# Weight squares in tiles of their own, weight blocks requested earlier, and TensorE in source order through the first down projection

## The chip, the core and the metric

One Trainium2 chip, one of its cores. The metric is the time in device microseconds of one execution of the whole program. The engines are named as the profile names them: PE (TensorE matmul), PEld (its weight loads), DVE (VectorE), ACT (ScalarE), POOL (GpSimd) and SP (SyncE, which here only issues DMAs).

## The reference

Windowed causal attention with a linear distance bias for 8 batches of 8 heads (576 positions, 64 dimensions), and then a bilinear feed-forward layer over the 4608 tokens that come out of it (512 channels, 1536 hidden). In short:

```python
scores = (q @ k.T) / sqrt(64) - slope[h] * |i - j|      # where 0 <= i - j < 128, else -1e9
attn   = exp(scores - max) ; attn /= attn.sum(-1) + 1e-9
x      = (attn @ v) transposed to (4608, 512)
out    = ((x @ w_a) * (x @ w_b)) @ w_out                # w_a, w_b: (512, 1536), w_out: (1536, 512)
```

The three weights come as float64 and everything else as float32. The result is wanted nearly as exact as float32, so the kernel writes the operands of most large products as a high and a low float16 part and takes three products (high x high, high x low, low x high). Each operand is first multiplied by a power of two, or near one, that is worked out from sums of squares.

## The kernel before

**Two streams.** One stream is the feed-forward work of a batch: `up` (the products with both up weights and their elementwise product, the tile `h`) and then `down` (the product with `w_out`). The other is the attention of the next batch, in pairs of heads, four pairs a batch. `att.along(main, n, place)` interleaves the two: after each step of the main stream it advances the attention to a place in proportion. Batch 0 differs: its attention runs first and alone (`first_attention`), then come `first_up` (49 steps) and `first_down` (24 steps), beside which the attention of batch 1 runs.

**The weights.** They pass through a third stream, `weights`, a generator advanced in small steps by whoever is in charge: 1.5 steps per step of the first attention, 50 in steps 0 to 39 of `first_up`, 12 in the first 12 steps of `first_down`, and the rest behind it. One chunk is two blocks of 512 KB; there are 12 chunks of up weights and 6 of `w_out`. For each chunk:

- `load_weights` issues two DMAs from SP (L121) into one of three raw places (`raws`, which lie in the tile `wdn`, not yet used for its own data).
- `convert` turns the 64-bit words into float32 on DVE in three operations (L132, L134, L135). The result goes to one of nine places in the tile `wsum`.
- `squares` (ACT, L141) writes the squares as bfloat16. Up to now they go over the raw words of the same chunk, so the raw place stays taken until the squares have been read.
- For an up chunk, `up_norms` sums the squares on PE (L157, `wn_ps`), `up_scales` makes the scales, and `split_up` (ACT L149, DVE L150) writes the two float16 parts to `wup`. The load of chunk n+3 is written behind `up_norms` of chunk n.
- For `w_out`, the sums of squares are added up, cast (DVE L102) and summed over the partitions by one matmul (PE L103, `wtot`). From that DVE makes `ratio` (L227), and only then are the 12 blocks split into `wdn`, high part on ACT (L231) and low part on DVE (L232). All products of `first_down` read `wdn`.

**The attention of one pair.** `scores` (PE into `sc_ps`: L380 for batch 1, L384 for later ones), the maximum with the bias (DVE L388) and the exponential (ACT L389), then `normalize`, which writes the probabilities as two float16 parts into the one tile `phl` (ACT L405, DVE L406), then `transpose_probs`, a transposing DMA from SP into `pT` (L411), then `pv` (PE L507 into `x_ps`, which `keep_x` empties on ACT at L420). `lay_out_qk` issues four copies on SP (L352 to L355) that bring a pair's split queries and keys into the places from which `scores` reads them. `load_v` (SP, L273) brings the values of a whole batch.

**What sets the order.** The scheduler arranges each engine's instructions by a simulation of its own, unless an engine is under `manual_schedule`; then they stay in the order in which the source issues them. Before, SP is manual through `first_attention` and all of `first_batch` (which holds `first_up`, `first_down` and the weights), and PE is manual from batch 1 on. `first_down` has four accumulating PSUM banks open at once (`dn_ps`, PE L818), and each of its first 12 steps gives 12 products to them.

```python
weave(att.along(first_up(st, h), 49, 3.2), (weights, 0, 40, 50))
weave(att.along(first_down(0, out_scale(st), h), 24, 5.15), (weights, 0, 12, 12))
```

Of the kernel before, what the change touches and what calls it, by code (L numbers as in the profile page):

```python
# [13 lines left out]
BF16 = mybir.dt.bfloat16  # L14
# [8 lines left out]
DM, DF = 512, 1536  # L23
P = 128
NPAIR = H // 2
NKC = DM // P
NF = DF // P
# [19 lines left out]
def attention_then_bilinear_ffn(ctx: ExitStack, tc: tile.TileContext, qT, kT, vP, w_a, w_b, w_out, rel, slopes2, outT):  # L47
# [40 lines left out]
    flat = wsum.rearrange("p f a c k q -> p (f a c k q)").bitcast(F32)  # L88
    forms = [flat[:, 2 * DM * n:2 * DM * n + 2 * DM].rearrange("p (m f) -> p m f", m=2) for n in range(9)]
    xs = const.tile([P, 8, 2, 2, HT], F16, name="xs")  # L90
    sup = const.tile([P, NF, 2], F32, name="sup")
# [46 lines left out]
    def squares(n, **kw):  # L138

        sq = raws[n % 3].bitcast(BF16)[:, :, 0:512]  # L140
        act.activation(sq, forms[n % len(forms)], AF.Square, **kw)  # L141
        return sq
# [16 lines left out]
    def up_scales(g, ps):  # L159
# [4 lines left out]
        power_scale(sup[:, 2 * g:2 * g + 2, :].rearrange("p f m -> p (f m)"), top, 1.01, 14, pool)  # L164

    def up_weights():

# [3 lines left out]
        for f in range(NF + 2):  # L171
            conv = convert(f) if f < NF else iter(())
            next(conv, None)
            n = f - 1
            if 0 <= n < NF:
                if n % 2 == 0:
                    ps = ps_at.tile([P, 512], F32, tag="at", name="wn_ps")
                up_norms(n, sq.pop(n), ps)
                if n + 3 < NF:
                    load_weights(n + 3, (w_a[n + 3], w_b[n + 3]), sp)  # L180
                else:
                    k = 2 * (n + 3 - NF)
                    load_weights(n + 3, (w_out[k], w_out[k + 1]), sp)
            yield
            next(conv, None)
            if rest:
                rest.pop(0)()
# [17 lines left out]
    def down_weights():  # L205

        sums = small.tile([P, NF // 2], F32, tag="wos", name="wos", bufs=1)
        for n in range(NF // 2 + 1):
            conv = convert(NF + n) if n < NF // 2 else iter(())
            next(conv, None)  # L210
            yield
            next(conv, None)
            if n:
                squares(NF + n - 1, accum_out=sums[:, n - 1:n])
                if n + 2 < NF // 2:
                    load_weights(NF + n + 2, (w_out[2 * n + 4], w_out[2 * n + 5]), sp)
            yield
# [801 lines left out]
    def first_batch():  # L1019
        st = states[0]  # L1020
        weave(att.along(first_up(st, h), 49, 3.2), (weights, 0, 40, 50))
        weave(att.along(first_down(0, out_scale(st), h), 24, 5.15), (weights, 0, 12, 12))
        for _ in weights:
            pass
# [12 lines left out]

    with tc.manual_schedule(engines={mybir.EngineType.PE}):
        for b in range(1, B):
            batch(b)  # L1040
# [40 lines left out]
```

## Time and profile before

| | before |
|---|---|
| Median of 3 runs | 992.15 us (991.67 to 992.97) |
| Profiled execution, its own time | 989.81 us |
| Span of that execution | 988.0 us |
| PE busy | 962.1 us (97%) |
| DVE busy | 669.0 us (68%) |
| ACT busy | 635.6 us (64%) |
| Granted PE clock, mean | 0.995 |

Some 26 us of the span are without a matmul. To find them the span is read in stretches: the first 58 us are the first attention, then `first_up` to about 153 us, `first_down` to about 200 us, and the seven other batches after that. Times in a timeline are counted from the start of the span; in its brackets stands how long the engine was idle before the instruction and what ended the wait.

### The profile page before, as it was taken

Reading aid. Unit: us, or ns where it says so; the run is one execution under the profiler, and the core shown is the slowest. Engines: PE = TensorE matmul, PEld = TensorE weight load, DVE = VectorE, ACT = ScalarE, POOL = GpSimd, SP = SyncE. Lnnn points to the kernel's source line nnn. Section 1 sums busy time; section 2 is a strip of 40 time slices with the busy share of each in tenths; the row PEclk is TensorE's granted clock in tenths of the full one; section 3 lists DMA queues with packets and bytes.
Section 4 is the critical chain, followed back from the end, with each engine's and each line's share of the span. In section 5 each row is a group of like instructions: output and inputs, shape, how many; then the busy total and the mean of one; then the engine's idle time right before and its main releaser. Section 6 shows DMA issues by size and latency. Waiting matters only on the chain.

```text
span 988.0 us, 23867 instructions
## 1 busy us (share of the span) xinstructions
PE 962.1 (97%) x9339; PEld 748.9 (76%) x9339; DVE 669.0 (68%) x1867; ACT 635.6 (64%) x1729; POOL 255.3 (26%) x309
## 2 busy tenths in 40 slices
PE   7899999999999999999999999999999999999998
PEld 5567777677777777777777777777777777877776
DVE  5979998668688657777778677757776576514520
ACT  5977769667676667766767766777667766413321
POOL 1211122032546313541225222211232012311100
PEclk8999999999999999999999999999999999999999
DMA  8434753664337234463345362373245432200001
GB/s 333 168 126 172 231 154 67 151 158 92 80 74 183 68 69 87 107 172 75 68 92 121 120 118 65 87 191 84 59 84 117 133 74 38 55 34 5 1 13 36
DMA packets 148432, 102.82 MB, mean 104 GB/s; under 512 B 120032, under 2 KB 128352, under 8 KB 147296
## 3 DMA queue, kind: packets, MB, share of 16 engines
q1 hardware_dynamic: 138816, 91.77, 38.2%
q10 hardware_dynamic: 9504, 9.54, 3.0%
q8 instruction: 73, 1.20, 0.5%
q14 instruction: 39, 0.32, 0.1%
HBM read 48.33 MB, written 9.44 MB: 58 GB/s over the span
## 4 chain that ended last, share of the span: by engine, by line
PE 69%; DVE 12%; ACT 7%; DMA 7%; issue 3%; POOL 1%; SPq 0%; ACTq 0%; DVEq 0%
PE ch L856 19%; PE dn_ps L952 18%; PE p L856 14%; PE up_ps L856 9%; PE x_ps L507 4%; DMA v<-in_vP 4%; PE sc_ps L384 3%; DVE phl L406 2%; PE dn_ps L818 2%; ACT t L389 1%; DVE wsum L135 1%; DVE xs L442 1%; ACT phl L405 1%; DVE wsum L134 1%; DMA qk<-in_kT 1%
## 5 line engine op out<-in xcount | busy, mean ns | idle before, releaser
L856 PEld LDWEIGHTS <-wup 128*128 128x128 f16 x3072 | 296.3, 98 | 82.0 <-issue 5.7
L952 PE MATMUL dn_ps<-h,wdn 128*128 128x288 f16 x2016 | 254.4, 286 | 0.0
L952 PEld LDWEIGHTS <-wdn 128*128 128x128 f16 x2016 | 193.9, 98 | 52.0 <-issue 0.2
L856 PE MATMUL up_ps<-xs,wup 128*128 128x288 f16 x1536 | 194.6, 286 | 1.1 <-ACT rc L867 0.8
L856 PEld LDWEIGHTS <-wsum 128*128 128x128 f16 x1152 | 111.7, 98 | 32.0 <-issue 2.5
L911 POOL TENSOR_TENSOR rc<-rc,row 128x288 f32<-128x288 f32 x64 | 62.3, 974 | 279.8 <-DVE row L909 263.9
L389 ACT ACTIVATE t<-t,mn 128x192 f32<-128x192 f32 (+2 forms) x252 | 107.2, 427 | 24.5 <-DVE mn L388 24.4
L856 PE MATMUL ch<-xs,wup 128*128 128x288 f16 x768 | 115.0, 286 | 0.5 <-ACT row L893 0.5
L856 PE MATMUL p<-xs,wup 128*128 128x288 f16 x768 | 115.1, 286 | 0.0
L406 DVE SCALAR_TENSOR_TENSOR phl<-t,rin,phl 128x192 f16<-128x192 f32 (+2 forms) x252 | 104.6, 454 | 15.3 <-ACT phl L405 15.1
L856 PE MATMUL ch<-xs,wsum 128*128 128x288 f16 x768 | 111.5, 286 | 1.1 <-ACT rc L881 1.1
L848 ACT CAST h<-rc 128x576 f16<-128x576 f32 x96 | 64.1, 668 | 69.1 <-DVE rc L916 37.2
L405 ACT ACTIVATE phl<-t,rin 128x192 f16<-128x192 f32 (+2 forms) x252 | 88.9, 425 | 25.3 <-DMA pT<-phl 12.7
L849 DVE TENSOR_TENSOR h<-rc,h 128x576 f16<-128x576 f32 x90 | 69.5, 772 | 30.5 <-ACT h L848 29.7
L388 DVE CUSTOM_DVE_ANT_0 t<-sc_ps,bias,neg 128x192 f32<-128x192 f32 (+2 forms) x216 | 73.9, 389 | 7.6 <-PE sc_ps L384 7.5
L957 ACT ACTIVATE row<-dn_ps,oi 128x288 f32<-128x288 f32 x56 | 27.6, 493 | 55.9 <-PE dn_ps L952 55.9
L893 ACT ACTIVATE row<-ch,g 128x288 f32<-128x288 f32 x64 | 31.8, 497 | 48.9 <-PE ch L856 48.9
L442 DVE TENSOR_TENSOR xs<-v,xs 128x576 f16<-128x576 f32 x52 | 47.8, 935 | 21.4 <-ACT xs L441 21.3
L888 DVE TENSOR_TENSOR rc<-p,rc 128x288 f32<-128x288 f32 x64 | 29.1, 454 | 44.3 <-PE p L856 34.7
L365 POOL TENSOR_SCALAR bias<-rel_sb,ninv,sl_sb 128x192 f32<-128x192 f32 x24 | 20.0, 832 | 147.8 <-DVE mn L388 129.8
L856 PE MATMUL p<-xs,wsum 128*128 128x288 f16 x384 | 57.5, 286 | 0.0
L436 POOL TENSOR_TENSOR xq<-xq,sq 128x576 bf16<-128x576 bf16 x22 | 29.2, 1325 | 75.7 <-ACT sq L435 75.7
(155 smaller groups left out, 1386.1 us busy)
## 6 DMA issues: line engine op xcount, KB each, us to landing
v<-in_vP SPq DMA_DIRECT2D x8, 1280.0 KB, 6.2
out<-row ACTq DMA_DIRECT2D x62, 144.0 KB, 1.8
qk<-in_qT SPq DMA_DIRECT2D x28, 288.0 KB, 4.0
qk<-in_kT SPq DMA_DIRECT2D x28, 288.0 KB, 4.4
wdn<-in_w_a SPq DMA_DIRECT2D x12, 512.0 KB, 5.1
wdn<-in_w_b SPq DMA_DIRECT2D x12, 512.0 KB, 6.1
wdn<-in_w_out SPq DMA_DIRECT2D x12, 512.0 KB, 4.6
qst<-qkh SPq DMA_DIRECT2D x24, 144.0 KB, 2.7
```

The lines of the kernel that those rows point to most:

```text
L388: vec.tensor_tensor_reduce(out=t[:, c:c + w], in0=ps[:, c:c + w], in1=o.bias[:, WIN - w:WIN], scale=-0.125 if o.b == 1 else o.neg, scalar= ...
L389: act.activation(t[:, c:c + w], t[:, c:c + w], AF.Exp, bias=o.mn[:, n:n + 1], scale=-1.0, accum_out=o.sm[:, n:n + 1])
L405: act.activation(phl[:, 0, pc:pc + w], e, AF.Copy, scale=s)
L406: vec.scalar_tensor_tensor(out=phl[:, 1, pc:pc + w], in0=e, scalar=s, in1=phl[:, 0, pc:pc + w], op0=ALU.mult, op1=ALU.subtract)
L442: vec.tensor_tensor(out=xs[:, n, 1, :, :], in0=src, in1=xs[:, n, 0, :, :], op=ALU.subtract)
L507: last = pe.matmul(xp[oc // 512][64 * h:64 * h + 64, o0:o0 + w], vt[0:rows, c:c + 64], probs(pt, rows, blocks, h), start=(n == 0 and first ...
L848: act.copy(h[:, f, :, 0, :], hid)
L849: eng.tensor_tensor(out=h[:, f, :, 1, :], in0=hid, in1=h[:, f, :, 0, :], op=ALU.subtract)
L856: pe.matmul(ps[:, 0:HT], w[:, wi, k, :], xs[:, b, xi, k, :], start=(first and n == 0), stop=(last and n == len(ks) - 1), skip_group_check= ...
L893: last_read[0] = last_main[0] = act.activation(mid, ch, AF.Copy, scale=st.g)
L911: pool.tensor_tensor(out=x0, in0=x0, in1=mid, op=ALU.mult)
L952: pe.matmul(ps[:, 0:HT], wdn[:, f, wi, e * P:(e + 1) * P], h[:, f, t, hi, :], start=(m == 0 and n == 0), stop=(m == NF - 1 and n == 2))
```

## The change

- The squares of the weights no longer go over the raw words. They go to three places of their own in turn: two halves of a tile `wsq` and a tile `wsq2`. These share their storage, by their tags, with the attention's `qk` and `qst` tiles, of which there is one each.
- The load of chunk f+3 is issued right after `convert` of chunk f, since only `convert` still reads the raw words.
- Four steps of `weights` run before `first_up`, 50 during it as before, and all that remain before `first_down`. None is left beside `first_down`.
- `first_down` leaves the stretch in which SP is manual and enters the one in which PE is manual.

Lines move: before's L141, L231, L273, L300, L389, L405, L411, L420, L507, L818 and L856 are L144, L238, L280, L307, L396, L412, L418, L427, L514, L825 and L863 after the change, and L352 to L355 are L359 to L362.

```diff
+    wsq = work.tile([P, 2, 2, DM], BF16, tag="qk", name="wsq")
+    wsq2 = work.tile([P, 2, DM], BF16, tag="qst", name="wsq2")
+    places = [wsq[:, 0], wsq[:, 1], wsq2]
...
     def squares(n, **kw):
-        sq = raws[n % 3].bitcast(BF16)[:, :, 0:512]
+        sq = places[n % 3]
         act.activation(sq, forms[n % len(forms)], AF.Square, **kw)
...
+    def load_raw(n):
+        if n < NF:
+            load_weights(n, (w_a[n], w_b[n]), sp)
+        elif n < NF + NF // 2:
+            k = 2 * (n - NF)
+            load_weights(n, (w_out[k], w_out[k + 1]), sp)
...
                 up_norms(n, sq.pop(n), ps)
-                if n + 3 < NF:
-                    load_weights(n + 3, (w_a[n + 3], w_b[n + 3]), sp)
-                else:
-                    k = 2 * (n + 3 - NF)
-                    load_weights(n + 3, (w_out[k], w_out[k + 1]), sp)
             yield
             next(conv, None)
+            if f < NF:
+                load_raw(f + 3)
...
             yield
             next(conv, None)
+            if n < NF // 2:
+                load_raw(NF + n + 3)
             if n:
                 squares(NF + n - 1, accum_out=sums[:, n - 1:n])
-                if n + 2 < NF // 2:
-                    load_weights(NF + n + 2, (w_out[2 * n + 4], w_out[2 * n + 5]), sp)
...
     def first_batch():
         st = states[0]
+        for _ in range(4):
+            next(weights)
         weave(att.along(first_up(st, h), 49, 3.2), (weights, 0, 40, 50))
-        weave(att.along(first_down(0, out_scale(st), h), 24, 5.15), (weights, 0, 12, 12))
         for _ in weights:
             pass
...
     with tc.manual_schedule(engines={mybir.EngineType.PE}):
+        for _ in att.along(first_down(0, out_scale(states[0]), h), 24, 5.15):
+            pass
         for b in range(1, B):
             batch(b)
```

How the instructions then stand on three engines. The rows give line, operation, what is written and read, its size, and how many in a row.

ACT, around the splits of `w_out` and the probabilities (`phl`) of the third pair of batch 1. Before, seven of that pair's nine `phl` instructions (the first of them is just above these rows) stand ahead of the splits, and two behind ten of them:

```order
L405 ACTIVATE phl<-t,rin 128x128
L405 ACTIVATE phl<-t,rin 128x192 x5
L848 CAST h<-rc 128x2x288
L792 COPY rc<-up_ps 128x288
L326 ACTIVATE qkl,qs<-qk 128x1152
L389 ACTIVATE t,sm<-t,mn 128x192 x2
L231 ACTIVATE wdn<-wsum,ratio 128x512 x9
L420 ACTIVATE v<-x_ps 128x512
L231 ACTIVATE wdn<-wsum,ratio 128x512
L300 ACTIVATE vhl<-v,sv 128x640
L420 ACTIVATE v<-x_ps 128x64
L405 ACTIVATE phl<-t,rin 128x192 x2
```

After:

```order
L238 ACTIVATE wdn<-wsum,ratio 128x512 x9
L427 ACTIVATE v<-x_ps 128x512
L238 ACTIVATE wdn<-wsum,ratio 128x512 x3
L307 ACTIVATE vhl<-v,sv 128x640
...
L427 ACTIVATE v<-x_ps 128x64
L855 CAST h<-rc 128x2x288
L412 ACTIVATE phl<-t,rin 128x64
L412 ACTIVATE phl<-t,rin 128x128
L412 ACTIVATE phl<-t,rin 128x192 x5
L799 COPY rc<-up_ps 128x288
L412 ACTIVATE phl<-t,rin 128x192 x2
```

In the gap stand two exponentials twice (L396), two copies of `rc` (L799), the squares of a pair's `qk` (L333), the squares of `x` (`xq`, L433), and a second `v<-x_ps` with its `vhl`. The splits and the `phl` instructions have changed places: now all 12 splits come ahead of all nine.

PE, where the third pair's `pv` starts. The number at the end of a tile's name tells the buffers apart. Before, `x_ps_2157` reads that pair's `pT`, and 104 products of `first_down` are ahead of it:

```order
L818 MATMUL dn_ps_2094<-h_787,wdn_122 128x288
L818 LDWEIGHTS wdn_122
L818 MATMUL dn_ps_2095<-h_787,wdn_122 128x288
L818 LDWEIGHTS wdn_122
L818 MATMUL dn_ps_2095<-h_787,wdn_122 128x288
L507 LDWEIGHTS vhl_2086
L507 MATMUL x_ps_2157<-pT_1991,vhl_2086 64x128
```

After, the same `pv` is `x_ps_2178`, and 24 products are ahead of it:

```order
L825 MATMUL dn_ps_2119<-h_791,wdn_122 128x288
L825 LDWEIGHTS wdn_122
L825 MATMUL dn_ps_2119<-h_791,wdn_122 128x288
L825 LDWEIGHTS wdn_122
L825 MATMUL dn_ps_2119<-h_791,wdn_122 128x288
L387 MATMUL sc_ps_2168<-qkl_1475,qkh_1474 64x192 x4
L514 LDWEIGHTS vhl_2096
L514 MATMUL x_ps_2178<-pT_2001,vhl_2096 64x128
```

The `pv` of the third pair has moved 80 products forward. The fourth pair's `pv` has 180 products ahead of it both times.

SP, at the layout copies for the first pair whose scores stand at the end of `first_down`. Before, the values of a batch (`v`) are requested behind the four copies and behind the transposing DMA:

```order
L352 DMA qst<-qkh 64x1152
L353 DMA qst<-qkl 64x1152
L354 DMA qkh<-qkh 64x1152
L355 DMA qkl<-qkl 64x1152
L316 DMA qk<-in_qT 64x2x576
L317 DMA qk<-in_kT 64x2x576
L411 DMA_TRANSPOSE pT<-phl 128x32x128
L273 DMA v<-in_vP 128x2560
```

After:

```order
L323 DMA qk<-in_qT 64x2x576
L324 DMA qk<-in_kT 64x2x576
L359 DMA qst<-qkh 64x1152
L360 DMA qst<-qkl 64x1152
L280 DMA v<-in_vP 128x2560
L361 DMA qkh<-qkh 64x1152
L362 DMA qkl<-qkl 64x1152
L418 DMA_TRANSPOSE pT<-phl 128x32x128
```

The load of `v` and the two loads of `qk` have come ahead of the last two layout copies and of the transposing DMA.

## Prediction

> **What bounds the kernel now.** I read the page first, then the table of stretches, then PE's waits up to 210 us, and last the timelines of PE, ACT, DVE and SP where those waits lie.
>
> ```profile
> span 988.0 us, 23867 instructions
> PE 962.1 (97%) x9339; PEld 748.9 (76%) x9339; DVE 669.0 (68%) x1867; ACT 635.6 (64%) x1729; POOL 255.3 (26%) x309
> ```
>
> PE is without a matmul for 988.0 - 962.1 = 25.9 us. No edit can bring more unless it removes matmuls, and this one removes none: both orders hold the same number of them. The stretches (columns: length, then busy time of PE, PEld, DVE, ACT and POOL, the granted clock, the DMA share and GB/s) show where those 25.9 us are.
>
> ```profile
> 12.00:19.00 7.00, 5.42 (x54) 4.20 (x56) 3.94 (x7) 6.44 (x18) 1.26 (x1) 0.52 1.03 406
> 26.00:29.00 3.00, 3.00 (x22) 2.27 (x23) 2.71 (x7) 1.74 (x8) 2.21 (x3) 0.50 0.83 299
> 30.00:60.00 30.00, 25.50 (x294) 17.20 (x294) 28.15 (x74) 27.79 (x79) 6.59 (x11) 1.00 0.30 106
> 76.00:140.00 64.00, 64.00 (x572) 48.87 (x570) 62.97 (x134) 44.70 (x114) 13.42 (x14) 1.00 0.62 193
> 140.00:150.00 10.00, 6.41 (x83) 4.93 (x81) 8.79 (x24) 7.52 (x18) 2.55 (x2) 1.00 0.25 59
> 150.00:160.00 10.00, 9.80 (x88) 7.29 (x90) 9.93 (x31) 10.00 (x25) 0.42 (x1) 1.00 0.01 2
> ```
>
> Behind 205 us both programs give PE the same order, so I take that part as it is. Between 76 and 140 us PE is never idle while DVE works 62.97 of 64 us: DVE keeps up, with nothing to spare. From 150 to 160 us ACT is busy for the whole 10.00 us and DVE for 9.93. PE's idle time between 76 and 205 us is three waits.
>
> ```profile
> PE wtot L103 <- DVE c L102: 2.4, 1, 2.4
> PE x_ps L507 <- DMA pT<-phl: 2.4, 1, 2.4
> PE sc_ps L380 <- issue: 1.4, 1, 1.4
> ```
>
> 2.4 + 2.4 + 1.4 = 6.2 us is all that the move of the weight work and the new order of the first down projection can take away here. The timeline of PE places them:
>
> ```profile
> 131.46 12.42 PE L856 MATMUL up_ps<-xs,wup 128*128 128x288 f16 x100
> 146.32 0.18 PE L103 MATMUL wtot<-c,ones 128*128 128x1 bf16 x1 [2.44 <-DVE c L102]
> 150.20 0.88 PE L380 MATMUL sc_ps<-qkl,qkh 64*64 64x64 f32 x12 [1.36 <-issue]
> 153.47 0.90 PE L818 MATMUL dn_ps<-h,wdn 128*128 128x288 f16 x6
> 160.32 7.89 PE L818 MATMUL dn_ps<-h,wdn 128*128 128x288 f16 x63
> 168.14 1.54 PE L507 MATMUL x_ps<-pT,vhl 128*64 128x128 f16 x42
> 183.93 1.54 PE L507 MATMUL x_ps<-pT,vhl 128*64 128x128 f16 x42 [2.44 <-DMA pT<-phl]
> 198.06 0.22 PE L384 MATMUL sc_ps<-qkh,qst 128*64 128x64 f16 x2
> ```
>
> The row at 168.14 is the third pair's `pv`. It has no bracket: its `pT` was there when PE came. How close that was is in SP's timeline and in the source view of the transposing DMA.
>
> ```profile
> 160.65 4.84 SPq L411 DMA_TRANSPOSE pT<-phl  x1
> DMA to landing us min/median/max: 6.7/6.9/9.2
> ```
>
> Issued at 160.65, a transposition of 6.7 us lands at 167.35, 0.8 us before PE wanted it. So this pair's probabilities were just on time, because 104 products of the down projection stood in front.
>
> **The change, part by part.**
>
> *Squares in their own places, earlier loads, four steps up front.* No work is added; the instruction counts are the same. The earlier loads could only help where DVE waits for a weight block, and nearly all of its time in the first 60 us is work: of 30 us from 30 to 60 it is busy for 28.15. What the four steps do is put conversion ahead of the last exponentials of the first attention: ten chunks stand there instead of eight.
>
> ```profile
> L135 DVE SCALAR_TENSOR_TENSOR wsum<-wdn,wsum 128x1024 uint32<-128x1024 uint32 x8 | 9.7, 1210 | 0.0
> L134 DVE SCALAR_TENSOR_TENSOR wsum<-wdn,wsum 128x1024 int32<-128x1024 int32 x7 | 8.6, 1231 | 0.1
> L132 DVE TENSOR_SCALAR wsum<-wdn 128x1024 int32<-128x1024 int32 x7 | 5.9, 842 | 2.4 <-DMA wdn<-in_w_b 2.3
> 62.50 0.94 DVE L628 SCALAR_TENSOR_TENSOR v<-x_ps,sv,rin 128x512 f32<-128x512 f32 x2 [4.32 <-PE x_ps L507]
> ```
>
> Two chunks are 2 x (1.21 + 1.23 + 0.84) = 6.6 us of DVE. Some of it fills the 4.32 us in which DVE waits at 62.50, so the start of `first_up` slips by between 6.6 - 4.32 = 2.3 and 6.6 us; I take 3.7, nearer the low end, since other work of DVE moves behind at the same place. The later `wtot` gives it back. In the new order `wtot` stands 99 matmuls earlier on PE, and 3.1 us of DVE's work (an operation of a conversion and a few smaller rows, by the order and the means of their groups) is no longer ahead of its cast. The cast was at 146.11; less the 3.1 and less about 3 of the 4.32 that are now filled, it comes at 140 (bounds 138.7 with all of it filled, 143.0 with none). The 99 are 53 of the up projection at 0.124 us (12.42 for 100), the 42 of a `pv` (1.54) and four scores (at most the 0.88 at 150.20): 9.0 us. PE gets there at 146.32 - 2.44 - 9.0 + 3.7 = 138.6, so some 1.4 us of that wait stay. The `ratio` follows within about 1 us, at 141.
>
> ```profile
> 146.11 0.15 DVE L102 CAST c<-wo 128x1 bf16<-128x1 f32 x1
> 145.55 2.35 ACT L405 ACTIVATE phl<-t,rin 128x64 f16<-128x64 f32 x7
> 150.75 5.61 ACT L231 ACTIVATE wdn<-wsum,ratio 128x512 f16<-128x512 f32 x9
> 159.84 0.74 DVE L406 SCALAR_TENSOR_TENSOR phl<-t,rin,phl 128x192 f16<-128x192 f32 x2
> ```
>
> *The third pair's probabilities.* Before, ACT made seven of the nine at 145.55, ahead of the splits. After, all 12 splits and other work stand in front. From `ratio` to the last `phl`, ACT's new order holds 12 splits at 5.61/9 = 0.62 us (7.5), the nine `phl` at 2.35/7 = 0.34 (3.0), and other work whose groups from 143 to 170 us are these (the last row is the page's):
>
> ```profile
> L389 ACT ACTIVATE t<-t,mn 128x192 f32<-128x192 f32 x7 | 3.1, 450 | 0.0
> L389 ACT ACTIVATION_READ_ACCUMULATOR t<-t,mn 128x1 f32 x9 | 1.7, 193 | 0.0
> L420 ACT ACTIVATE v<-x_ps 128x512 f32<-128x512 f32 x2 | 1.2, 586 | 0.4 <-PE x_ps L507 0.4
> L326 ACT ACTIVATE qkl<-qk 128x1152 bf16<-128x1152 f32 x1 | 1.2, 1162 | 0.0
> L300 ACT ACTIVATE vhl<-v,sv 128x640 f16<-128x640 f32 x1 | 0.8, 817 | 0.0
> L405 ACT ACTIVATE phl<-t,rin 128x192 f16<-128x192 f32 (+2 forms) x252 | 88.9, 425 | 25.3 <-DMA pT<-phl 12.7
> ```
>
> Four exponentials with their sums (2.6), two `x` out of PSUM (1.2), the squares (1.2), two `vhl` (1.6) and seven small rows taken at 0.4 (2.8) are 9.4 us in means. In a row means overlap: seven `phl` took 2.35 us where seven means of 0.425 are 2.98. Between that 0.8 and 0.9 it is some 8.0, and with the rest 18.5 us. DVE has nearly as much there (12 low parts, nine `phl`, two `vhl`), and I let it end 1.2 us behind ACT. So `phl` is complete at 141 + 19.7 = 160.7, against 159.84 + 0.74 = 160.6 before, and `pT` lands 6.8 later, at 167.5. The earlier `ratio` is spent on the splits.
>
> *TensorE in the source's order.* The same `pv` now stands behind 24 products instead of 104. PE's first product comes at about 140.2 + 9.0 (the 99 matmuls) + 5.8 (153.47 - 146.32 less the 1.36 idle) = 155.0. The 24 products take 24 x 0.1253 (7.89 us for 63) = 3.0, the scores and the sum between them 1.8, and the fourth bank may hold them up to 2.5 us longer, since an `rc` copy on ACT (L799) that frees it stands behind the splits too. PE is at the `pv` by 160 to 162 and waits until 167.5: some 6 us. Behind it wait, in PE's own queue, the 80 products that used to cover the transposition, 80 x 0.1253 = 10.0 us. In exchange the fourth pair's `pv` comes later, and its 2.44 us at 183.93 go: with 156 products (19.5 us) and some scores between the two it is reached at about 191, while its `pT` landed by 183.93 before and would have to be 7 us later to hold PE up. Against the row at 168.14 the sum is (167.5 - 168.14) + 10.0 - 2.44 = +6.9 us. The waits at `wtot` and at 150.20 are inside this sum: whatever PE saves there it waits for at the `pv`.
>
> *SP's new order.* SP leaves the manual stretch at the first down projection. The load of `v` moves ahead of the last two layout copies and the transposing DMA.
>
> ```profile
> 192.09 1.31 SPq L355 DMA_DIRECT2D qkl<-qkl  x1
> DMA to landing us min/median/max: 3.5/3.5/3.5
> 202.12 0.58 SPq L273 DMA_DIRECT2D v<-in_vP  x1
> v<-in_vP SPq DMA_DIRECT2D x8, 1280.0 KB, 6.2
> qk<-in_kT SPq DMA_DIRECT2D x28, 288.0 KB, 4.4
> ```
>
> The last copy lands at 192.09 + 3.5 = 195.6 and the scores that read it start at 198.06, so they have 2.5 us in hand. The load costs SP 0.58 us if the DMA engines serve it beside the copies (no loss) and 6.2 us if the copies wait until it has landed (a loss of 3.7). No row tells which; I take the middle, +1.8. Should the scores be late, nothing else on PE comes first: they are next in its fixed order. The two loads of `qk` that move ahead as well can wait for the last square in `wsq`; what is queued behind them on SP, the third pair's transposition, wants `phl` at 160.7 and is later anyway, so I cost it at nothing. Without that cover it would cost a landing, the 4.4 us of their row.
>
> **The sum.** 6.9 + 1.8 = +8.7 us against the profiled execution: 989.81 + 8.7 = 998.5. That execution is 2.34 us faster than the median of the runs, 992.15, so on that median I predict 1000.8.
>
> **A rule on the clock.** In the stretches above the granted clock is 0.52 from 12 to 19 us, where PE is busy for 5.42 of 7.00, and 0.50 from 26 to 29 us, behind idle gaps; from 30 us on it is 1.00 in every one, although PE then waits 2.44 us twice. Nothing here shows a clock after a wait of 6 us. As a mechanism of this kernel: if PE's clock halves in that wait and stays so for 3 to 7 us, as long as in the two rows, half of that time is lost, +1.5 to +3.5. The Trainium skill, "TensorE: Matmul & The Clock Gate", section "Part 1: The HAM clock gate", states such a rule: the clock drops to half after one idle window of about 3.4 us and comes back after about as long of sustained work. [...]
>
> **Rivals.**
>
> *A, the other side: the third pair's `pT` is there in time.* If ACT got to the `phl` rows without waiting for the splits, both waits for `pT` would be gone, and with them 2.44 us, and parts of 2.44 and 1.36 in front, less the slip of the start: 989.81 - 2.44 - 1.36 - 2.44 + 3.7 = 987.3, on the median 989.6. It decides at a landing before 158.6: 168.14 - 10.0 + 2.44 - 2.0. For that `phl` must be complete by 151.8, and `ratio` be there by 132. The order on ACT and the bound of 138.7 speak against it. Chance 0.05.
>
> *B, half of it.* The splits overlap better than before, `pT` lands at 164, and `v` costs nothing: (164 - 168.14) + 10.0 - 2.44 = +3.4, on the median 995.6. ACT at 10.00 of 10.00 us in 150 to 160 speaks against it. For it speaks that the seven small rows, 2.8 us, are only estimated, and that the cast may come at 138.7. Chance 0.12.
>
> *C, the halved clock* on top of the main case: 1000.8 + 1.5 to 3.5, about 1003.3. For it the rows at 12 and 26 us, against it the rows after 30. Chance 0.18.
>
> *D, no change.* The scheduler's moves cancel, within 2 us. It would take `pT` landing at about 160.6 with `v` free. Chance 0.05.
>
> **How the numbers follow.** The likeliest case is the sum, chance 0.60, and its time is my prediction, 1000.8. Runs of this kernel differ so that 0.2%, about 2 us, is as little as can be told from no change. The main case's own range takes `pT` at 165.5 to 169.5 and `v` at 0 to 3.7: (165.5 - 168.14) + 7.6 = +5.0 to (169.5 - 168.14) + 7.6 + 3.7 = +12.7, or 997.1 to 1004.8. Taking in most of B and of C, the range is 995.5 to 1004.5. A is the faster side with 0.05, D the same with 0.05, and the main case, B and C are slower with 0.90.
>
> **What would show it.** Right: a wait of 4 to 8 us at the first `x_ps` behind 24 products of the down projection, at 160 to 168 us, put down to the DMA into `pT`; no wait at the fourth pair's; `wtot` at 139 to 143 with a wait of 0 to 3; `first_up` starting some 3.7 us later; a wait of 0 to 4 at the scores that read `qst` near the end of the down projection. Wrong: ACT's `phl` rows complete before 155, the `pv` without a bracket, or PE idle where the order of before had none, such as at a `dn_ps` bank for more than 2.5 us. A clock below 1.00 in the 4 us behind the `pv` would show C.

## The result: slower by 1.43%, and by more than forecast

| | before | after |
|---|---|---|
| Median | 992.56 us (4 runs, three of them those above, 991.67 to 994.25) | 1006.82 us (4 runs, 1005.15 to 1007.93) |
| Ratio | | 1.0143, 95% interval 1.0119 to 1.0167 |
| Profiled execution | 989.81 us | 1007.72 us |
| Span | 988.0 us | 1005.9 us |

The forecast was 1000.8 us with a range from 995.5 to 1004.5, 8.7 us above the kernel before; measured are 14.3 between the medians. The sign was right, the time lies above the range. A second series of the changed kernel, beside other runs of the kernel before, gave 1007.72 us against 991.00 (1.0167, 1.0152 to 1.0182).

The five of PE's waits in the first 230 us of the changed kernel that matter here (columns: engine, line, what ended the wait; total, times, longest):

```profile
PE x_ps L514 <- DMA pT<-phl: 7.0, 1, 7.0
PE tr_ps L601 <- ACT t L595: 4.7, 6, 1.5
PE dn_ps L825 <- ACT rc L799: 3.1, 1, 3.1
PE sc_ps L391 <- DMA qkl<-qkl: 0.8, 1, 0.8
PE wtot L106 <- DVE c L105: 0.8, 1, 0.8
```

The waits forecast are there: 7.0 us for the third pair's `pT`, 3.1 for the fourth bank, 0.8 at the scores behind the load of `v`; the wait at `wtot` has shrunk from 2.4 to 0.8. PE's timeline places them.

```profile
68.48 1.97 PE L514 MATMUL x_ps<-pT,v 128*64 128x128 f32 x28
143.80 0.18 PE L106 MATMUL wtot<-c,ones 128*128 128x1 bf16 x1 [0.77 <-DVE c L105]
158.41 1.27 PE L825 MATMUL dn_ps<-h,wdn 128*128 128x288 f16 x9
163.62 0.88 PE L825 MATMUL dn_ps<-h,wdn 128*128 128x288 f16 x3 [3.07 <-ACT rc L799]
174.72 2.77 PE L514 MATMUL x_ps<-pT,vhl 128*64 128x128 f16 x42 [7.00 <-DMA pT<-phl]
177.42 4.33 PE L825 MATMUL dn_ps<-h,wdn 128*128 128x288 f16 x24
200.03 1.51 PE L514 MATMUL x_ps<-pT,vhl 128*64 128x128 f16 x42
215.35 0.22 PE L391 MATMUL sc_ps<-qkl,qst 128*64 128x64 f16 x2 [0.78 <-DMA qkl<-qkl]
216.11 1.64 PE L825 MATMUL dn_ps<-h,wdn 128*128 128x288 f16 x12
```

Two things here go beyond the sum. The last `x_ps` of the first attention begins at 68.48 us; it began at 60.53 before. And the `pv` behind the long wait took 2.77 us instead of 1.54, and the next 24 products 4.33 instead of the 3.1 at which they run elsewhere. The kernel before has at these places, and for its last group of the down projection:

```profile
60.53 1.97 PE L507 MATMUL x_ps<-pT,v 128*64 128x128 f32 x28
195.03 3.10 PE L818 MATMUL dn_ps<-h,wdn 128*128 128x288 f16 x24
198.85 1.64 PE L818 MATMUL dn_ps<-h,wdn 128*128 128x288 f16 x12
```

**A ledger of PE.** The last group of the first down projection (12 products) begins at 198.85 us before and at 216.11 after, 17.3 later, and almost all of the 17.9 us between the two profiled executions is there. Up to that point PE has the same matmuls to do (the records hold 1793 and 1794 of them). So the difference must be time in which PE had nothing, or ran at half clock. Stretches of both kernels, before first (columns as in the prediction; the granted clock stands third from the end):

```profile
0.00:72.00 72.00, 61.43 (x629) 43.70 (x630) 54.16 (x151) 53.08 (x147) 14.54 (x38) 0.93 0.55 203
140.00:198.85 58.85, 52.62 (x559) 40.15 (x558) 43.43 (x137) 43.51 (x115) 9.11 (x9) 1.00 0.49 105
```

```profile
0.00:72.00 72.00, 57.73 (x559) 40.46 (x560) 53.02 (x135) 47.42 (x132) 13.23 (x35) 0.83 0.56 207
140.00:216.11 76.11, 64.35 (x655) 48.91 (x654) 47.39 (x145) 50.05 (x131) 10.63 (x10) 0.91 0.53 116
```

Idle time is length less busy time. The clock loss is busy time x (1 - granted clock), added up over stretches of 1 us. Both in us:

| | 0 to 72: idle | 0 to 72: clock | 140 to the mark: idle | 140 to the mark: clock | mark |
|---|---|---|---|---|---|
| before | 10.6 | 4.4 | 6.2 | 0.0 | 198.85 |
| after | 14.3 | 10.2 | 11.8 | 3.9 | 216.11 |

Of the 19.0 us, half (9.5) was lost in the first 72 us and half (9.5) behind 140 us; what is left as work is 177.6 and 175.9 us. Between 72 and 140 us neither loses anything. By kind, 9.3 us are idle time and 9.7 us are half clock. The ledger closes to 1.7 us (19.0 against 17.3).

It is a ledger of two single executions, which lie 17.9 us apart where the medians lie 14.3 apart. The one of before has a high mean clock (0.995; its other executions on record have 0.988 to 0.997), the changed one a low one (0.981 of 0.980 to 0.988). A part of the 9.7 us may therefore belong to these two executions and not to the change.

### The profile page after: what moved, and what is told of

The parts are those of the page before. It is cut to its first block, busy times and chain, and to the rows that moved or that the text cites. A ratio compares the mean times of both kernels' runs of the same rounds, so it can differ in the third digit from the quotient of the medians.

```text
span 1005.9 us, 23842 instructions
## 1 busy us (share of the span) xinstructions
PE 970.4 (96%) x9339; PEld 754.3 (75%) x9339; DVE 670.4 (67%) x1867; ACT 637.1 (63%) x1729; POOL 255.2 (25%) x309
## 4 chain that ended last, share of the span: by engine, by line
PE 76%; DVE 10%; DMA 6%; ACT 5%; issue 2%; SPq 0%; POOL 0%; ACTq 0%; DVEq 0%
PE ch L863 19%; PE dn_ps L959 18%; PE up_ps L863 15%; PE p L863 14%; PE x_ps L514 4%; PE sc_ps L391 3%; PE dn_ps L825 3%; DMA v<-in_vP 2%; DVE phl L413 2%; DVE xs L449 1%; DMA wdn<-in_w_b 1%; DMA qk<-in_kT 1%; DVE t L395 1%; PE sc_ps L387 1%; DVE wsum L267 1%
## 5 line engine op out<-in xcount | busy, mean ns | idle before, releaser
L863 PEld LDWEIGHTS <-wup 128*128 128x128 f16 x3072 | 296.4, 98 | 81.6 <-issue 5.5
L863 PE MATMUL up_ps<-xs,wup 128*128 128x288 f16 x1536 | 195.1, 286 | 0.3 <-DVE v L635 0.3
L863 PEld LDWEIGHTS <-wsum 128*128 128x128 f16 x1152 | 111.7, 98 | 32.8 <-issue 3.2
L396 ACT ACTIVATE t<-t,mn 128x192 f32<-128x192 f32 (+2 forms) x252 | 107.2, 427 | 27.0 <-DVE mn L395 26.9
L413 DVE SCALAR_TENSOR_TENSOR phl<-t,rin,phl 128x192 f16<-128x192 f32 (+2 forms) x252 | 107.5, 466 | 15.8 <-ACT phl L412 15.5
L863 PE MATMUL ch<-xs,wup 128*128 128x288 f16 x768 | 115.0, 286 | 0.5 <-ACT row L900 0.5
L863 PE MATMUL p<-xs,wup 128*128 128x288 f16 x768 | 115.1, 286 | 0.0
L863 PE MATMUL ch<-xs,wsum 128*128 128x288 f16 x768 | 111.5, 286 | 1.9 <-ACT rc L888 1.9
L412 ACT ACTIVATE phl<-t,rin 128x192 f16<-128x192 f32 (+2 forms) x252 | 88.8, 425 | 24.5 <-DMA pT<-phl 12.4
L856 DVE TENSOR_TENSOR h<-rc,h 128x576 f16<-128x576 f32 x90 | 69.5, 773 | 30.3 <-ACT h L855 29.5
L863 PE MATMUL p<-xs,wsum 128*128 128x288 f16 x384 | 57.6, 286 | 0.0
L514 PE MATMUL x_ps<-pT,vhl 128*64 128x128 f16 (+2 forms) x1176 | 44.0, 232 | 7.0 <-DMA pT<-phl 7.0
```

The lines of the kernel that those rows point to most:

```text
L396: act.activation(t[:, c:c + w], t[:, c:c + w], AF.Exp, bias=o.mn[:, n:n + 1], scale=-1.0, accum_out=o.sm[:, n:n + 1])
L412: act.activation(phl[:, 0, pc:pc + w], e, AF.Copy, scale=s)
L413: vec.scalar_tensor_tensor(out=phl[:, 1, pc:pc + w], in0=e, scalar=s, in1=phl[:, 0, pc:pc + w], op0=ALU.mult, op1=ALU.subtract)
L514: last = pe.matmul(xp[oc // 512][64 * h:64 * h + 64, o0:o0 + w], vt[0:rows, c:c + 64], probs(pt, rows, blocks, h), start=(n == 0 and first ...
L856: eng.tensor_tensor(out=h[:, f, :, 1, :], in0=hid, in1=h[:, f, :, 0, :], op=ALU.subtract)
L863: pe.matmul(ps[:, 0:HT], w[:, wi, k, :], xs[:, b, xi, k, :], start=(first and n == 0), stop=(last and n == len(ks) - 1), skip_group_check= ...
```

## Experiments

Three theories at the outset. *Order*: the loss is the third pair's `pv` in PE's fixed order, behind 24 products. *Drain*: the loss comes from the splits of `w_out`, which now all stand ahead of `phl` on ACT, wherever the `pv` stands. *Start*: the loss begins in the first attention, where DVE does conversions ahead of the exponentials. Each run is compared with runs of the kernel before on the same chip.

**1. The order undone in the changed kernel.**

```diff
         for _ in weights:
             pass
+        for _ in att.along(first_down(0, out_scale(st), h), 24, 5.15):
+            pass
...
     with tc.manual_schedule(engines={mybir.EngineType.PE}):
-        for _ in att.along(first_down(0, out_scale(states[0]), h), 24, 5.15):
-            pass
```

> The changed kernel with one part undone: the first down projection is arranged by the scheduler again (SP manual there, PE not), the weights still all drained ahead of it. The third pair's pv then stands behind 96 products instead of 24. Theory order (the loss is the pv's place in PE's fixed order): PE reaches the pv at about 176.6 us, two us after its pT lands, the 7.0 us wait and the 2.6 us of half clock behind it are gone, 1006.8 - 9.6 = about 997 us. Rival drain (the loss comes from the splits ahead of phl, wherever the pv stands): pT is late all the same and other work cannot cover it, 1003 us or more. Rival start (all of it is the late start): unchanged, 1006.

Measured 1003.57 us, 1.0120 (1.0104 to 1.0137) of before. Only 2 to 5 us of the 14 to 17 came back. The wait at the third pair's `pv` fell to 2.0 us, but the fourth pair's then took 5.7:

```profile
173.70 2.23 PE L514 MATMUL x_ps<-pT,vhl 128*64 128x128 f16 x42 [2.02 <-DMA pT<-phl]
196.76 2.77 PE L514 MATMUL x_ps<-pT,vhl 128*64 128x128 f16 x42 [5.71 <-DMA pT<-phl]
```

The order alone isn't the loss: neither its 997 us nor the 1006 of *start* was met. The number of *drain*, 1003 us or more, was: the third pair's `pT` came at 173.7 us, nearly as late as the 174.7 of the changed kernel, and other work covered its wait only in part.

**2. The pv pushed back within the source order.**

```diff
-        for _ in att.along(first_down(0, out_scale(states[0]), h), 24, 5.15):
+        down0 = first_down(0, out_scale(states[0]), h)
+        for _ in range(6):
+            next(down0)
+        for _ in att.along(down0, 18, 5.15):
             pass
```

> The changed kernel with PE still in source order, but the attention is not advanced in the first 6 of the 24 steps of the first down projection, so that the third pair's pv stands behind 96 products instead of 24. Theory order: the same gain as from undoing the manual order, about 997 us (996 to 999), the 3.1 us wait for the fourth bank stays. Rival drain: 1003 or more. If the manual order itself costs something beyond the pv's place, this run stays above the scheduled one by that much.

Measured 1007.67 us, 1.0170 (1.0149 to 1.0190): nothing won, and again *drain*'s number. The `pv` no longer waits, and the wait has moved to the end of the projection, into scores whose attention now has 18 steps instead of 24:

```profile
PE sc_ps L391 <- DMA qkl<-qkl: 5.6, 1, 5.6
PE dn_ps L825 <- ACT rc L799: 3.1, 1, 3.1
PE sc_ps L391 <- DVE mn L395: 2.5, 1, 2.5
```

**3. No early steps.**

```diff
     def first_batch():
         st = states[0]
-        for _ in range(4):
-            next(weights)
```

> The changed kernel without the four early steps of the weights. On ACT seven of the third pair's nine phl instructions then stand ahead of the splits of w_out, as before; its pv still stands behind 24 products. Theory order plus start: first_up starts near 63 us again, wtot near 143 to 146 us, pT lands at 161 to 164 us, the wait at the pv shrinks from 7.0 to 1 to 4 us: (163 - 168.1) + 10.0 - 2.4 = +2.4 us on 992.5, about 995 (994 to 999). Rival that the start costs nothing because DVE's total of work sets wtot: pT lands as late as in the changed kernel and the time stays at 1005 to 1008.

Measured 1001.43 us, 1.0107 (1.0089 to 1.0125): a gain of 4 to 6 us, less than expected. The third pair's `pv` began at 170.58 after a wait of 1.9, but the last `x_ps` of the first attention still began at 65.92.

Without the early steps seven of the third pair's nine `phl` stand ahead of the splits on ACT again, and this shows what is right in *drain*. From the start of `wtot` to SP's issue of that pair's transposition it is 17.0 us in this run (146.51 to 163.48), 24.1 in the changed kernel (143.80 to 167.87) and 14.3 before (146.32 to 160.65). In all profiled executions of this document it is 22.9 to 24.4 us where the 12 splits come first (the changed kernel in both series, runs 1, 2, 4, 10 and 12), and 14.3 to 17.3 where seven `phl` do (before, and all the others). The order on ACT is thus worth some 6 to 10 us of `pT`'s date.

**4. The wait filled.**

```diff
     def pv(p, st, o, vhl):
         xp = new_x_ps()
+        if o.b == 1 and o.p == 2:
+            for _ in range(90):
+                pe.matmul(xp[0][:, 0:P], ones16, ones16, start=True, stop=True, skip_group_check=True)
```

> The changed kernel with 90 small matmuls of ones (128 columns, bf16) put ahead of the third pair's pv, into the PSUM bank that the pv overwrites; they fill the wait for pT and change no result. Theory clock (the pv and the next 24 products ran at half the clock because PE had waited): the granted clock stays at 1.00 behind the pv, the pv takes 1.5 instead of 2.8 us and the 24 products 3.0 instead of 4.3, 1006.8 - 2.6 = about 1004. Rival (they were slow for another reason, a transfer or the weights): 1006 to 1008.

Measured 1003.54 us, 1.0124 (1.0108 to 1.0141), against 1.0143 and 1.0167 for the changed kernel in its two series. PE's timeline with the filled wait:

```profile
166.31 5.20 PE L521 MATMUL x_ps<-ones 128*128 128x128 bf16 x90
173.14 1.54 PE L514 MATMUL x_ps<-pT,vhl 128*64 128x128 f16 x42 [1.63 <-DMA pT<-phl]
174.60 3.12 PE L828 MATMUL dn_ps<-h,wdn 128*128 128x288 f16 x24
```

The `pv` takes 1.54 us again and the 24 products 3.12. The half clock behind the long wait cost 1.23 + 1.21 = 2.4 us.

**5. Own places only, loads at their old place.** The changed kernel without the early steps, and with `load_raw` behind `up_norms`.

```diff
                 up_norms(n, sq.pop(n), ps)
+                load_raw(n + 3)
...
-            if f < NF:
-                load_raw(f + 3)
...
```

The loads of `w_out` move back in the same way.

> The changed kernel without the four early steps and with the loads issued where they were before (behind up_norms); the squares keep their own places and PE its source order. Eight chunks are then converted ahead of the last x of the first attention, as before, against nine without the four steps and ten in the changed kernel. Theory start (each chunk converted ahead of that point delays first_up by 2.6 to 5.4 us, since DVE has no idle time there): the last x_ps of the first attention begins at 60 to 61.5 us again, against 65.9 with nine and 68.5 with ten. The rest of the loss is the third pair's pv behind 24 products: a wait of 3 to 7 us there, 997 to 1000 us. Rival that the start is not set by DVE's conversions: x_ps stays at 65 or later.

Measured 1001.56 us, 1.0114 (1.0085 to 1.0142). Eight chunks ahead of the last `x`, as before, and yet its `x_ps` began at 64.58. The count was the wrong one. Conversions had also come forward among the exponentials: 23 conversion operations ahead of the last exponential (at 55.5 us) instead of 21 (at 51.7), since a raw place no longer has to wait for its squares: before, SP's weight loads wait 28.2 us in all for `wn_ps`, which reads the squares, and in this run not at all. Runs 10 and 11 will show that this count does not explain the start either.

**6 and 7. Each half of the change alone**, on the kernel before: first own places and early loads, then only the first down projection under PE's source order, where, as in the change, SP is no longer manual (both without the early steps).

> The kernel before with only the squares in own places and the loads right behind convert (no early steps, the first down projection arranged by the scheduler with 12 weight steps beside it, as before). Nine chunks are converted early. Theory start: the last x_ps begins at about 66 us, 5.4 later than before; of that up to 3.8 come back as smaller waits at wtot and at the scores behind it, so 993 to 997. Rival that earlier loads and own places cost nothing: 991 to 992.5.

> The kernel before with only the order of the first down projection changed: PE manual there, with the 12 weight steps beside it. The start is untouched; the third pair's pv stands behind 24 products. Theory order, by the terms of the prediction: pT lands at 167.4, PE reaches the pv at 159 to 161, waits 6 to 8 us and runs up to 7 us at half clock behind it: (167.4 - 168.1) + 10.0 - 2.4 = +6.9 and +2.5 for the clock, 999 to 1001.5. Rival (the order is harmless, the start makes all the loss): 991 to 993.

The first measured 996.40 us, 1.0067 (1.0042 to 1.0092); the second 997.50, 1.0075 (1.0051 to 1.0098). So each half costs some 6 to 7 us by itself. With PE's order alone the wait lies mostly at the bank, not at the `pv`:

```profile
159.83 0.88 PE L818 MATMUL dn_ps<-h,wdn 128*128 128x288 f16 x3 [4.82 <-ACT rc L792]
160.58 3.04 PE L818 MATMUL dn_ps<-h,wdn 128*128 128x288 f16 x12
166.78 1.54 PE L507 MATMUL x_ps<-pT,vhl 128*64 128x128 f16 x42 [1.70 <-DMA pT<-phl]
```

4.82 + 1.70 = 6.5 us of waits, near the 6 to 8 expected at one place. The 12 products behind the first wait took 3.04 us, twice their 1.5.

**8. Fewer conversions early in the kernel before**: `first_attention(weights, 1.25)` and 54 steps beside `first_up`.

> The kernel before with four weight steps fewer in the first attention (1.25 steps a place instead of 1.5) and four more in the first up projection: seven chunks are converted ahead of the last x. Theory start, simple form: first_up begins 2.6 to 5.4 us earlier and the time falls by as much, 987 to 989. Rival that DVE's total of work up to wtot is the bound: first_up begins earlier, but the wait at wtot grows by as much, 991 to 993.

Measured 993.66 us, 1.0028 (1.0012 to 1.0043). Less early work does not help either: the last `x_ps` began at 60.44, as before, and `wtot` came 3 us later with a wait of 3.04 us. That DVE's work was only put off, and has to be done by `wtot` all the same, agrees with this, but no run separates it from other reasons.

**9 to 11. The conversions held back by order alone**, with everything else of each kernel left as it is. The changed kernel once more beside it (9), the hold in the changed kernel (10), and in the kernel of run 6 (11).

```diff
+    last_exp, last_x = [None], [None]
+    def gated(n):
+        g = last_x[0] if n >= 8 else last_exp[0] if n == 7 else None
+        return tc.issue_after(g.ins) if g else ExitStack()
...
-        vec.tensor_scalar(out=t, in0=high, ...)
+        with gated(n):
+            vec.tensor_scalar(out=t, in0=high, ...)
```

(`last_exp` and `last_x` are set where the first attention issues its exponentials' maxima and its `x` on DVE.)

> The changed kernel once more, unaltered, so that the next two runs are compared with it beside the same runs of the kernel before: +14 us on before (+12 to +16).

> The changed kernel with the conversion of chunk 7 held behind the last exponential of the first attention on DVE and that of chunks 8 and later behind its last x, by order alone: eight chunks stand ahead of the last x again. All else stays (own places, early loads, four steps, drained weights, PE in source order). Theory start (conversions pulled ahead are what makes the start late): the last exponential is at 51 to 52 us and the last x_ps at 60 to 61, against 57.6 and 68.5. wtot then comes at 138 to 140 and pT lands at 169 to 171 instead of 174.7, so 3.5 to 5 us are won, about 1002; the wait at the pv stays or grows, since PE arrives earlier still. Rival (the start is late for another reason, the loads for one): x_ps stays at 65 or later and the time at 1006.

> The kernel before with own places and early loads, no early steps, its own first down projection (run before at +6.0 us), and the same hold on the conversions. Theory start: the start is at 60 to 61 us again and the time back at that of the kernel before, within 2 us, or up to 2 us under it since wtot's squares are not held up by their places. Rival (the early loads or the places cost something else, by their DMAs or their shared tiles): it stays at +4 or more.

Run 9 measured 1007.72 us, 1.0167. Run 10 measured 1004.10, 1.0126 (1.0110 to 1.0142): 3.6 us won, as expected in size. Run 11 measured 991.00, 0.9999 (0.9986 to 1.0012): the 6 us of run 6 are gone. The reason that I gave is not borne out, though. The last `x_ps` began at 63.37 and 64.37, not at 60 to 61, and the last exponential's maximum at 54.9 and 55.6, with 21 conversion operations ahead of it, as many as in the kernel before, which has it at 51.7. The ledger (below) shows the loss at the start nearly as large as without the hold. What the hold changed in run 11 is the later part: behind 140 us PE loses 3.0 us where it lost 8.4 in run 6. The third pair's `pv` begins at the same time in both (169.71 and 169.73); the difference is the fourth pair's. In run 6 the scheduler put the squares of the next `qk` ahead of that pair's last four `phl` on ACT, and there they wait for a load; with the hold it put them behind. Run 6 first, then run 11:

```profile
177.30 1.16 ACT L333 ACTIVATE qkl<-qk 128x1152 bf16<-128x1152 f32 x1 [3.59 <-DMA qk<-in_kT]
178.47 1.48 ACT L412 ACTIVATE phl<-t,rin 128x192 f16<-128x192 f32 x4
190.04 2.77 PE L514 MATMUL x_ps<-pT,vhl 128*64 128x128 f16 x42 [4.37 <-DMA pT<-phl]
```

```profile
174.34 1.49 ACT L419 ACTIVATE phl<-t,rin 128x192 f16<-128x192 f32 x4 [0.75 <-DVE rin L416]
179.70 1.16 ACT L340 ACTIVATE qkl<-qk 128x1152 bf16<-128x1152 f32 x1 [3.88 <-PE dn_ps L832]
185.15 1.54 PE L521 MATMUL x_ps<-pT,vhl 128*64 128x128 f16 x42 [0.29 <-DMA pT<-phl]
```

So the 6 us of run 6 lie for the most part in this order on ACT, and at the start something else had to be left.

**12 to 14. The clock of the first attention.** What was open then: whether the half clock at the start is a cause or only goes with the waits.

```diff
             tp = ps_ef.tile([P, 512], F32, tag="ef", name="tr_ps")
+            for _ in range(10):
+                pe.matmul(tp[:, 0:P], ones16, ones16, start=True, stop=True)
```

> The changed kernel with ten small matmuls of ones (128 columns, bf16) ahead of each of the 16 groups of transposes in the first attention, written into the PSUM bank that the transposes overwrite: they fill gaps in which PE waits for the exponentials and change no result (the scheduler then also puts one chunk's conversion behind the last exponential: eight instead of nine). In the changed kernel PE loses some 6 to 10 us of work to the half clock in the first 72 us, before about 4. Theory clock at the start: the granted clock stays at 1.00 there, the last x_ps begins 3 to 6 us earlier, and the time falls by 2 to 4 us, less than the clock loss, since DVE sets much of the start: about 1003 to 1005 against 1007. Rival (DVE alone sets the start, a slow clock costs nothing there): no change, or 1 to 3 us slower by the added matmuls.

> The same added matmuls in the kernel before, where PE loses 4.4 us to the half clock in the first 72 us. Theory clock at the start: the last x_ps begins 1 to 3 us earlier; of that little is left, since DVE is busy nearly all the time to wtot: 989 to 991, same or up to 0.2% faster. Rival (the added matmuls lie on PE's path): 992 to 996.

> The same added matmuls in the kernel before with own places, early loads and the held conversions (equal to the kernel before without them; 7.5 us of half clock in the first 72 us). Theory clock at the start: up to 4 us won at the start and no wait at wtot to give it back to, 987 to 990. Rival (DVE alone sets the start): 991 to 993.

| | time | ratio to before | lost in 0 to 72 us: idle, clock | mark |
|---|---|---|---|---|
| 12, in the changed kernel | 1000.66 us | 1.0095 (1.0076 to 1.0114) | 8.5, 1.7 | 212.36 |
| 13, in the kernel before | 990.16 us | 0.9991 (0.9983 to 1.0000) | 5.7, 0.0 | 198.44 |
| 14, in the kernel of run 11 | 986.56 us | 0.9953 (0.9939 to 0.9967) | 5.8, 0.0 | 194.74 |

The added matmuls count as busy, so the idle time in this table can't be compared with that of the other kernels; the clock's loss and the dates can. In run 12 the median fell by 7.1 us against the second series of the changed kernel and by 4.8 against the first, in ratios to before. The mark moved by 3.5 to 3.8 us, which is the 2 to 4 expected; the rest lies behind it, where both kernels have the same work. The scheduler also left 24 instead of 27 conversion operations ahead of the last exponential there, so not all of it need be the clock. In the kernel before the matmuls won 0.7 us (interval 0 to 1.7): its last `x_ps` begins only 0.3 us earlier (60.24), and its `wtot` still waits 2.27 us for DVE. In run 14 they won 4.4 us, and that version is faster than both kernels. Its last `x_ps` begins at 60.06, as early as in the kernel before with the same matmuls; the fourth pair's `pv` no longer waits:

```profile
60.06 1.97 PE L521 MATMUL x_ps<-pT,v 128*64 128x128 f32 x28 [0.62 <-ACT rin L637]
179.36 1.51 PE L521 MATMUL x_ps<-pT,vhl 128*64 128x128 f16 x42
140.00:194.74 54.74, 53.13 (x565) 40.75 (x563) 40.69 (x133) 41.94 (x113) 9.38 (x9) 1.00 0.53 113
```

From 140 us to the mark it loses 1.6 us, against 6.2 before. So with the clock held up, own places and early loads cost nothing at the start, once the conversions are held back. The clock held up without the hold was not run in this kernel.

**The ledger of the runs without added matmuls** (idle and clock together, in us, one profiled execution each):

| kernel | 0 to 72 | 72 to 140 | 140 to the mark |
|---|---|---|---|
| before | 15.0 | 0.0 | 6.2 |
| 7, only PE's order | 14.7 | 0.0 | 15.8 |
| 8, fewer conversions early | 15.5 | 0.3 | 11.4 |
| 6, only own places and early loads | 18.7 | 0.4 | 8.4 |
| 11, the same with the hold | 19.5 | 0.0 | 3.0 |
| 5, own places and PE's order | 19.1 | 0.0 | 15.3 |
| 3, the change without early steps | 20.7 | 0.4 | 10.4 |
| 1, the change without PE's order | 23.9 | 0.1 | 12.9 |
| 2, the change with the `pv` pushed back | 23.4 | 0.0 | 17.5 |
| 10, the change with the hold | 20.8 | 2.8 | 13.2 |
| the change, first and second series | 24.5, 22.8 | 0.0, 0.0 | 15.7, 17.0 |

The left column falls into groups: about 15 us with the old weight places, 19 to 21 with places of their own, 23 to 24.5 with the four early steps as well (20.8 with the hold). In the right column PE's order alone adds 9.6 us. These three, some 4, some 4 and 9.6, come near the 19.0, but they are not its shares: run 1, without PE's order, still loses 12.9 on the right. How the loss divides among the parts of the change stays open; two executions of one kernel differ by up to 1.7 us in a column.

## Why the prediction went wrong, step by step

- **The direction and the mechanism held.** The wait came at the named instruction, the `pv` behind 24 products, put down to the DMA into `pT`, with 7.0 us (forecast some 6). The bank took 3.1 (up to 2.5; more than 2.5 us at a `dn_ps` bank was one of the prediction's signs of being wrong), the 80 products behind the `pv` came as written, and the fourth pair's 2.44 us vanished (its `pv` at 200.03 has no bracket).
- **The step that failed is the date of `pT`, "at 167.5"; it came at 174.7.** With the measured date the prediction's own formula gives (174.72 - 168.14) + 10.0 - 2.44 = +14.1 instead of +6.9. Four rows of the changed kernel carry the 7.2 us:

```profile
143.59 0.16 DVE L105 CAST c<-wo 128x1 bf16<-128x1 f32 x1
163.47 0.81 ACT L412 ACTIVATE phl<-t,rin 128x192 f16<-128x192 f32 x2
166.98 0.41 DVE L413 SCALAR_TENSOR_TENSOR phl<-t,rin,phl 128x192 f16<-128x192 f32 x1
167.87 4.83 SPq L418 DMA_TRANSPOSE pT<-phl  x1
```

- **Half of that, 3.6 us, is the cast: 143.6 instead of 140.** Behind it is the slip of `first_up`, put at 3.7 us; the last `x_ps` slipped by 68.48 - 60.53 = 7.95, over the upper bound of 6.6. Three things were wrong in it. The whole slip was put on the four early steps, and own places and earlier loads at nothing; but in run 6, which has no early steps, the last `x_ps` is already at 65.11, 4.6 us late, and with the loads at their old place (run 5) at 64.58. I also let the extra chunks fill DVE's 4.32 us of waiting at 62.50. But it did not fill up; it moved along and became 5.5, so it looks like the time that PE and ACT need from DVE's earlier results to the last `x` (it is 3.9 to 5.9 us in every run):

```profile
70.45 0.94 DVE L635 SCALAR_TENSOR_TENSOR v<-x_ps,sv,rin 128x512 f32<-128x512 f32 x2 [5.45 <-PE x_ps L514]
```

  And PE itself got slower there: its loss to the half clock in the first 72 us grew by 5.8 us (4.4 to 10.2), while its idle time grew by 3.7. In the second series it was 1.7 and 6.0, so the split between the two varies from execution to execution and the sum less (9.5 and 7.8).
- **ACT's stretch** from the first split to the last `phl` took 19.2 us (145.10 to 164.28) instead of 18.5; 1.1 of it is a wait for the load of `qk`, costed at nothing. **DVE** ended 3.1 us behind ACT (167.39) instead of 1.2, since it served other work of the next pair in between. SP issued the transposition 0.5 us later, and it took the 6.85 us expected.
- **The clock was a rival with a chance of 0.18 and came on top of the main case.** Behind the `pv` it cost 2.4 us (run 4), inside the 1.5 to 3.5 given. The Trainium skill, "TensorE: Matmul & The Clock Gate", section "Part 1: The HAM clock gate", has the clock halve after an idle window of about 3.4 us. The 7.0 us wait agrees with that: the granted clock was 1.00 until 169 us and 0.50 from 170. Other rows do not: it was also 0.50 from 164 to 166 us behind the 3.07 us wait for the bank, and at the start without any gap over 1.5 us (last section). The larger share of the clock's loss was at the start, 10.2 us against 3.9 behind 140, at a place that no step of the prediction looked at for it; with added matmuls there the mark came 3.5 to 3.8 us earlier (run 12).
- **SP's order** cost 0.8 us instead of 1.8, inside its bounds.
- **The sum as measured** is 14.1 + 2.4 + 0.8 = 17.3 us, which is by how much the mark moved.
- **"Whatever PE saves there it waits for at the `pv`"** held in part. The hold of run 10 took 2 to 4 us off the start's loss; of that 2.8 came back between 72 and 140 us, yet `wtot` and `pT` came earlier and the time fell by 3.6. What was missing is the other direction: what PE and DVE lose at the start moves `wtot`, and with it `pT`. In the seven executions with the splits ahead (both series of the change, runs 1, 2, 4, 10 and 12) the last `x_ps` begins between 63.05 and 68.48 us, and `wtot` follows it by 74.3 to 77.3 us each time.

## What to carry to other kernels

Work moved earlier on a saturated engine can delay what stands behind it there, however early its data are: look at what stands ahead of every instruction that another engine waits for, and don't let such work fill a gap that is another engine's latency chain hanging on the same engine's last result. The count alone isn't enough: runs 10 and 11 had the counts of the kernel before and still began 3 to 4 us late. A change of order on one engine is also a change in what the scheduler does on the others, as with ACT's `phl`. Keep a ledger of the limiting engine by stage (idle time, and busy time lost to a slow clock), for a single wait that is removed, as the `pv`'s in run 2, may only surface elsewhere. And where that engine works in short pieces, price its clock too: matmuls added in idle time won 4.4 us in run 14, but only 0.7 in the kernel before.

## What was not expected of the hardware

PE's clock halved without any long wait. In the changed kernel PE's longest gap with a named wait between 32 and 36 us is 0.62 us, four in a row (the fourth, of 0.32 us, ends at 35.82), and yet the granted clock is 0.79 from 36 to 37 us and 0.50 from then to 43:

```profile
32.73 0.44 PE L601 MATMUL tr_ps<-ident,t 128*128 128x128 f32 x2 [0.57 <-ACT t L595]
33.78 0.61 PE L160 MATMUL wn_ps<-wsq,ones 128*128 128x256 bf16 x4 [0.62 <-DVE mn L594]
34.90 0.60 PE L160 MATMUL wn_ps<-wsq,ones 128*128 128x256 bf16 x4 [0.51 <-ACT wsq L144]
36.00:37.00 1.00, 1.00 (x6) 0.41 (x6) 1.00 (x4) 1.00 (x6) 0.00 (x0) 0.79 1.05 430
38.00:39.00 1.00, 1.00 (x7) 0.50 (x3) 1.00 (x2) 0.31 (x1) 0.00 (x0) 0.50 0.00 0
```

The kernel before has the same at its start: the longest idle times of PE in its first 30 us are these two, and the granted clock was 0.50 from 13 to 19 us and from 26 to 29.

```profile
13.05 1.12 PE L594 MATMUL tr_ps<-ident,t 128*128 128x128 f32 x4 [1.50 <-ACT t L588]
24.07 0.33 PE L594 MATMUL tr_ps<-ident,t 128*128 128x128 f32 x1 [1.33 <-DVE mn L587]
```

In the 4 us ahead of the three falls PE was busy for 2.0 us (32 to 36, changed kernel), 1.3 (9 to 13) and 2.5 (22 to 26, both before). From 32 to 36 us of the kernel before it was busy for 2.7 us and the clock stayed at 1.00. No run here measures where the limit lies.

Ten added matmuls of ones in such gaps kept the clock at 1.00 through the whole first attention (runs 13 and 14). Behind the 7.0 us wait the clock came back only at about 180 us, 5 us after work had begun again at 174.72.
